# Convolution groups of twice the width, in the two small PSUM banks and in the PSUM pair of the output tile closed last

## The chip, the cores and the metric

The kernel runs on one core of a Trainium2 chip. A core has TensorE (PE in the profile, its weight loads PEld), VectorE (DVE), ScalarE (ACT), GpSimd (POOL) and SyncE (SP), which work through their own queues in order and wait for each other through semaphores, and 16 DMA engines. PSUM, into which TensorE writes, has 8 banks of 512 numbers of 32 bits in each of 128 partitions. The metric is the device time of one execution in microseconds (us); less is better.

## The reference

With S = 2048 rows, D = 576 channels and Dff = 4608:

```python
x = A_q
xn = _layernorm(x, axis=-1)
return x + _A_ref(xn, A_k, A_v, A_shift_k, A_ssm_k, A_ssm_D) + _B_ref(xn, B_w1, B_w2)

# A, of (q, k, v, shift_k, ssm_k, ssm_D), q being xn
k_shift = sum(k_pad[:, t:t + S, :] * shift_k[:, ks - 1 - t] for t in range(4))
kv = k_shift * v
y = causal_convolution_over_S(kv, ssm_k)      # per channel, through an FFT of length 2 S
A = q * (y + kv * ssm_D)

# B
h = maximum(einsum("bsd,df->bsf", x, w1), 0)
B = einsum("bsf,fd->bsd", h, w2)
```

(The two convolutions are written shorter here.) B is by far the larger part of the arithmetic; A's long convolution is a Fourier transform, a product and a way back, all as small matmuls.

## The kernel before

**Two streams on one TensorE.** The feed-forward part B is a fixed program: `QUADS` rounds (36), from the fourth on each a `quad` with seven products into the PSUM banks `psh` (tags h0, h1) and eight output units. The products come in the order 00, two units, 01, a rest, unit, s2, unit, s1, unit, s3, a rest, s4, two units, a rest, unit, 11, a rest. A product (`product`, L566) is two times three matmuls of 512 columns; a unit (`mm2`, L715) is 12 matmuls of 288 columns into a PSUM pair `pso`, two banks wide, which VectorE then adds to `acc` (L739; 21 units in the input stage are seeded by a ScalarE copy instead and copied back by it). `open_unit` (L707) opens the pair of the next unit before the matmuls of this one, so the two pairs take turns.

**The convolution** is a generator, `conv`, that is advanced between those pieces. `tick(cost)` (L1125) is called after each half of a product, each rest and each unit. It adds the cost to a clock, and while the convolution's clock is not behind it takes up to two steps, `next(stream)`. A step yields a weight (`W_FX` and the like), or a negative pause during which only B runs, so that transfers land. So the instructions of the convolution stand where tick happened to be called, in the middle of a product as well. `in_turn` (L750) holds its matmuls to this order on TensorE; `here` holds its copies behind the latest work of B on VectorE and ScalarE.

**Stages of the convolution**, each with 64-row matmuls in four quadrants (in the last, 128 rows by 64 columns) into the small banks `psf`, of which there are two (`fft_psum`):

- filter: 22 times `filter_group` of `KG` = 432 columns, through `group` (L807): matmuls into two banks, then a copy of one by ScalarE (L823) and of the other by VectorE (L825) into the ring `zs`, then stores to `zk` by SyncE (L861);
- input: 18 times `input_group` of `CW` = 512 columns, both copies by ScalarE, stores to `zx`; the rows before it are multiplied and gated on VectorE (`tap`, `gate`);
- frequency: for each of 18 pairs of chunks n a `spectrum` of the filter (four ScalarE copies, L994, then a swap of halves by DMA), a `product_of` (four VectorE multiplications, L1010, and a DMA into the one buffer `other`), a `join` (one VectorE instruction of 1024 columns, L1021, that reads `other`) and a `way_back` (two ScalarE copies, L1029, and stores to `zy`). In round n the order is spectrum n + 1, join n - 1, product n, way_back n - 1, with a weight yielded after the spectrum, the product and the way back;
- output: 16 tiles; two sets of matmuls of 288 columns, two `gate`s on VectorE (L1081), an `add` (L1088).

`Ring.put` gives the next of a few buffers; a buffer given again waits for its last readers.

## Time and profile before

| | |
|---|---|
| median of 3 runs | 1055.54 us (1054.64 to 1057.38) |
| the profiled execution's own time | 1057.48 us |
| its span in the profile | 1055.7 us |
| busy on VectorE | 700.0 us, 66% |
| busy on ScalarE | 435.6 us, 41% |
| busy on GpSimd | 464.4 us, 44% |
| line 752 on TensorE, the convolution's matmuls | 127.8 us, 1160 instructions |

The profile is one execution. In its rows "out<-in" are tiles (`psf` from `area`, the convolution's buffers; `pso` from `w` and `hh` or `ll`, a unit; `psh` from `x` or `xs` and a weight, a product), with partitions x columns. A matmul of the convolution (line 752) appears as two rows, one for each of two passes. Matmuls are pipelined, so a row's duration is longer than the distance to the next one: distances of starts are what counts on TensorE. An arrow in brackets says how long the engine had been idle and what ended that.

### The profile page before, as it was taken

The numbers are of one execution on the slowest core, as the hardware profiler recorded it, in microseconds if no ns is written. First come the engines' busy times: TensorE is split into PE (matmuls) and PEld (weight loads), VectorE is DVE, ScalarE is ACT, GpSimd is POOL, SyncE is SP. The second block draws the span as 40 slices with busy tenths as digits, with TensorE's granted clock in tenths as the row PEclk, the third lists the DMA queues.
The fourth block names the chain that finished last, engine by engine and source line by source line (L and its number), as shares of the span: only waits on it lengthen the run. The fifth ranks groups of instructions, "written<-read, shape, count | busy, mean of one in ns | idle before, by whom it ended". The sixth has DMA issues, their size and how long they took to land.

```text
span 1055.7 us, 17578 instructions
## 1 busy us (share of the span) xinstructions
PE 1038.6 (98%) x6506; PEld 844.5 (80%) x6506; DVE 700.0 (66%) x1083; ACT 435.6 (41%) x813; POOL 464.4 (44%) x502
## 2 busy tenths in 40 slices
PE   9999999999999999999999999999999999999997
PEld 5898999998877879888788888766766666678777
DVE  6787777774555547788778877456655566655765
ACT  7244334443435344444444444444344434433220
POOL 3335455555444354555454546423243224335351
PEclk9999999999999999999999999999999999999999
DMA  6114374579354563389942443597887677746785
GB/s 178 54 48 122 109 160 133 175 208 187 82 169 142 175 211 102 115 265 318 272 143 95 133 139 113 184 211 208 241 226 213 200 230 223 210 133 202 245 271 150
DMA packets 136321, 184.70 MB, mean 175 GB/s; under 512 B 70333, under 2 KB 88639, under 8 KB 135340
## 3 DMA queue, kind: packets, MB, share of 16 engines
q1 hardware_dynamic: 81652, 123.48, 39.3%
q0 software_dynamic: 16048, 52.44, 16.4%
q10 hardware_dynamic: 38536, 7.66, 3.8%
q8 instruction: 51, 0.84, 0.3%
q14 instruction: 34, 0.28, 0.1%
HBM read 119.04 MB, written 45.61 MB: 156 GB/s over the span
## 4 chain that ended last, share of the span: by engine, by line
PE 87%; DVE 5%; DMA 3%; ACT 2%; issue 2%; ACTq 1%; SPq 0%; DVEq 0%
PE pso L562 39%; PE psh L562 33%; PE psf L752 10%; PE psh_c L562 3%; DMA area<-area 2%; DVE area L1010 1%; DVE ll L586 1%; PE psw L1163 1%; DMA zk<-area 1%; DMA zy<-area 1%; DVE area L1021 1%; ACT area L994 1%; DVE acc L739 1%; ACTq L799 0%; DVE area L909 0%
## 5 line engine op out<-in xcount | busy, mean ns | idle before, releaser
L562 PE MATMUL pso<-w,hh 128*128 128x288 f32 x2304 | 468.0, 296 | 0.7 <-DVE acc L739 0.7
L562 PEld LDWEIGHTS pso<-w,hh 128*128 128x128 f32 x2304 | 378.4, 188 | 38.3 <-issue 10.8
L562 PE MATMUL pso<-w,ll 128*128 128x288 f32 x1152 | 339.4, 295 | 0.0
L739 DVE TENSOR_TENSOR acc<-pso,acc 128x576 f32<-128x576 f32 x243 | 183.0, 754 | 189.6 <-PE pso L562 189.2
L562 PEld LDWEIGHTS pso<-w,ll 128*128 128x128 f32 x1152 | 216.2, 188 | 0.0
L506 POOL TENSOR_TENSOR wb<-sums,wb 128x512 fp32r<-128x512 f32 x33 | 51.7, 1567 | 288.7 <-ACT wb L505 246.5
L506 POOL TENSOR_TENSOR w<-r,w 128x576 fp32r<-128x576 f32 x72 | 106.7, 1488 | 130.8 <-ACT w L505 130.8
L752 PE MATMUL psf<-area 64*64 64x512 f32 (+10 forms) x1160 | 127.8, 472 | 3.8 <-PE psh L562 1.4
L562 PE MATMUL psh<-x,wa 128*128 128x512 f32 x396 | 105.8, 399 | 3.3 <-ACT psh L641 3.2
L562 PE MATMUL psh<-xs,wb 128*128 128x512 f32 x396 | 106.2, 400 | 1.1 <-ACT u L656 1.1
L562 PEld LDWEIGHTS psh<-x,wa 128*128 128x128 f32 x396 | 71.5, 188 | 26.7 <-issue 9.1
L562 PEld LDWEIGHTS psh<-xs,wb 128*128 128x128 f32 x396 | 69.7, 188 | 26.5 <-issue 13.7
L562 PE MATMUL psh<-hl,wr 128*128 128x512 f32 x264 | 83.9, 399 | 0.4 <-ACT p L662 0.4
L506 POOL TENSOR_TENSOR wa<-r,wa 128x512 fp32r<-128x512 f32 x36 | 58.7, 1629 | 52.1 <-ACT wa L505 52.0
L586 DVE SCALAR_TENSOR_TENSOR ll<-psh,hh 128x512 fp32r<-128x512 f32 x66 | 45.2, 685 | 53.5 <-ACT hh L584 53.5
L752 PEld LDWEIGHTS psf<-area 64*64 64x64 f32 (+1 forms) x1160 | 39.6, 132 | 47.0 <-issue 25.2
L584 ACT ACTIVATE hh<-psh 128x512 fp32r<-128x512 f32 x66 | 39.5, 598 | 75.9 <-PE psh L562 75.7
L584 ACT ACTIVATE hh<-p 128x512 fp32r<-128x512 f32 x33 | 20.9, 632 | 103.0 <-DVE p L684 58.7
L677 DVE TENSOR_TENSOR u<-psh,u 128x512 f32<-128x512 f32 x33 | 22.8, 691 | 55.6 <-PE psh L562 53.0
L562 PEld LDWEIGHTS psh<-hl,wr 128*128 128x128 f32 x264 | 47.0, 188 | 14.6 <-issue 6.0
L679 ACT ACTIVATE psh<-psh 128x512 f32<-128x512 f32 x33 | 19.2, 582 | 93.9 <-DVE u L677 93.9
L562 PE MATMUL psh<-x,wc 128*128 128x512 f32 x198 | 53.9, 402 | 0.0
(127 smaller groups left out, 1454.3 us busy)
## 6 DMA issues: line engine op xcount, KB each, us to landing
r<-in_w POOLq DMA_DIRECT2D x70, 288.0 KB, 3.8
area<-area SPq DMA_DIRECT2D x144, 128.0 KB, 4.3
r<-in_w POOLq DMA_DIRECT2D x35, 512.0 KB, 4.6
area<-zk SPq DMA_DIRECT2D x18, 512.0 KB, 4.6
area<-zx SPq DMA_DIRECT2D x18, 512.0 KB, 3.3
zy<-area SPq DMA_DIRECT2D x36, 256.0 KB, 4.2
area<-zy SPq DMA_DIRECT2D x32, 288.0 KB, 5.0
zk<-area SPq DMA_DIRECT2D x42, 144.0 KB, 2.2
```

Of the source, the lines that this page charges most:

```text
L506: nc.gpsimd.tensor_tensor(w[:, 1, :n], src, w[:, 0, :n], OP.subtract)
L562: last = nc.tensor.matmul(ps, a, m, start=start and n == 0, stop=n == len(seq) - 1, skip_group_check=True)
L584: done["act"] = nc.scalar.activation(hh, ps, AF.Relu)
L586: nc.vector.scalar_tensor_tensor(ll, ps, 0.0, hh, op0=OP.max, op1=OP.subtract)
L677: nc.vector.tensor_tensor(u2, x, u2, OP.add)
L679: nc.scalar.activation(x, y, AF.Copy, scale=-1.0)
L739: done["acc"] = nc.vector.tensor_tensor(two(acc[t]), ps[:, :, :NH], two(acc[t]), OP.add)
L752: done["pe"] = nc.tensor.matmul(ps, a, m, start=start, stop=stop)
L994: nc.scalar.activation(filt[:, c, k, :], banks[k], AF.Copy)
L1010: nc.vector.tensor_tensor(filt[:, c, k, :], banks[k], filt[:, c, k, :], OP.mult)
L1021: nc.vector.scalar_tensor_tensor(filt, other, sign, filt, op0=OP.mult, op1=OP.add)
L1163: last = nc.tensor.matmul(idle[0], warm[:, :P], warm, start=True, stop=True)
```

## The change

`group` now takes two parts. The first goes into the two small banks as before, the second into a pair `psg` of the tag that held the output tile closed last (`borrowed`). The pairs `pso` get a tag each (`o0`, `o1`), and `slot` remembers which was opened and which closed last. Filter and input groups hold twice the columns: 11 and 9 of them, the last filter group shorter in its second part. In the frequency stage product n and spectrum n + 1 stand together, the spectrum in the borrowed pair, copied by two ScalarE instructions of 1024 columns instead of four of 512; way_back follows the product after 5.6 weights, not 3.6. In the output stage two tiles go together.

Before each such group the stream yields "wide"; `tick` then takes no step until it is called with `place` true, which is not so in the middle of a product and after a unit. The ring `zs` holds two wide buffers, the length of one group, instead of four half ones, of two groups. `terms` shrinks to one buffer, `sums` grows to four; the output stage has four rows of lookahead instead of three. A pair whose borrowed columns are fewer than a unit's is kept from being seeded (`unwritten`).

```diff
-    ps_o = ctx.enter_context(tc.tile_pool(name="ps_o", bufs=2, space=PSUM))
+    ps_o = ctx.enter_context(tc.tile_pool(name="ps_o", bufs=1, space=PSUM))
...
+    slot = {"open": 0, "closed": 0}
+    unwritten = set()
+
+    def borrowed():
+
+        return ps_o.tile([P, 2, 512], F32, tag=f"o{slot['closed']}", name="psg")
+
...
             matmuls(ps, ((h, hi), (h, lo), (l, hi)), start and c == 0)
-            tick(3 * W_MM)
+            tick(3 * W_MM, c == 1)
...
-        ps = open_ps[g, t] = ps_o.tile([P, 2, 512], F32, tag="o", name=f"pso{g}_{t}")
-        if seed:
+        slot["open"] = 1 - slot["open"]
+        ps = ps_o.tile([P, 2, 512], F32, tag=f"o{slot['open']}", name=f"pso{g}_{t}")
+        open_ps[g, t] = ps, slot["open"]
+        if seed and slot["open"] not in unwritten:
             seeded.add(t)
             nc.scalar.activation(ps[:, :, :NH], two(acc[t]), AF.Copy)
...
-        ps = open_ps.pop((g, t))
+        ps, slot["closed"] = open_ps.pop((g, t))
+        unwritten.discard(slot["closed"])
...
-        tick(W_UNIT)
+        tick(W_UNIT, False)
...
-        zs = Ring(*views(Z, 4, CW))
+        zs = Ring(*views(Z, 2, 2, CW))
...
+        def group(parts, engines):
+
+
+            wide = borrowed()
+            sets = [[fft_psum() for _ in range(2)], [wide[:, r, :] for r in range(2)]]
+            ends = []
+            for pieces, banks in zip(parts, sets):
+                off = 0
+                for w, mat, src in pieces:
+                    for k in range(2):
+                        for r in range(2):
+                            in_turn(banks[r][sides[r ^ k], off:off + w],
+                                    mat(r)[sides[r], A1 * (r ^ k):A1 * (r ^ k) + A1],
+                                    src[sides[r]], off == 0, True)
+                    off += w
+                ends.append(off)
+            if ends[-1] < NH or len(ends) == 1:
+                unwritten.add(slot["closed"])
+            outs = []
+            for n, off in enumerate(ends):
+                out = zs.put(("z", n))
+                outs.append([out[:, r, :] for r in range(2)])
+                if n and engines == ("act", "act"):
+                    with here():
+                        nc.scalar.activation(out[:, :, :off], wide[:, :, :off], AF.Copy)
+                    continue
+                for r in range(2):
+                    with here():
+                        if engines[r] == "act":
+                            nc.scalar.activation(out[:, r, :off], sets[n][r][:, :off], AF.Copy)
+                        else:
+                            nc.vector.tensor_copy(out[:, r, :off], sets[n][r][:, :off])
+            return outs
...
-            while starts and min(starts[0] + KG, flat) <= e * NH + (e == A2 - 1) * NH:
+            while starts and min(starts[0] + 2 * KG, flat) <= e * NH + (e == A2 - 1) * NH:
+                yield "wide"
                 filter_group(starts.pop(0))
-                yield W_FK / 2 / (len(range(0, flat, KG)) / A2)
+                yield W_FK / 2 / (len(range(0, flat, 2 * KG)) / A2)
...
-        sums = Ring(*rows[11:14])
-        terms = Ring(*rows[14:16])
+        sums = Ring(*rows[11:15])
+        terms = Ring(*rows[15:16])
...
-                    while made_groups < n_groups and (made_groups * CW + CW - 1) // D <= last:
+                    while made_groups < n_groups and (2 * CW * (made_groups + 1) - 1) // D <= last:
+                        yield "wide"
                         input_group(made_groups)
                         made_groups += 1
-                        yield W_FX
+                        yield 2 * W_FX
...
+        def second_spectrum(n):
+            wide = borrowed()
+            return spectrum(n, [wide[:, k, :] for k in range(2)], lambda to: [(to, wide)])
 
         def product_of(n):
 
             banks = [fft_psum() for _ in range(2)]
             turn(banks, [(0, raw["x"][n])])
             filt = filters[n]
+            leave = second_spectrum(n + 1) if n + 1 in pairs_n else lambda: None
...
+            leave()
...
-        spectrum(0)
+        first_spectrum()
         yield W_FMK
         for n in range(NCH // 2 + 1):
             if n + 1 in pairs_n:
-                spectrum(n + 1)
-            if n <= NCH // 2:
-                yield W_FMK
+                yield "wide"
             if n:
                 join(n - 1)
-            if n == NCH // 2:
-                yield W_FMX
             if n in pairs_n:
                 product_of(n)
-                yield W_FMX
+            yield W_FMK / 2 + W_FMX
             if n:
                 way_back(n - 1)
-                yield W_FMB
+                yield W_FMK / 2 + W_FMB
...
-        for i, t in enumerate(order):
-            y = ys.put(i)
-            banks = [fft_psum() for _ in range(2)]
+        for i in range(0, T, 2):
+            yield "wide"
+            wide = borrowed()
+            sets = [[fft_psum() for _ in range(2)], [wide[:, h, :] for h in range(2)]]
+            y = {j: ys.put(j) for j in (i, i + 1)}
+            for j, banks in zip(y, sets):
+                for h in range(2):
+                    for u in range(U):
+                        in_turn(banks[h][halves(u)[0], :NH], invs[j][:, u, :],
+                                zos[j, u][:, h * NH:(h + 1) * NH], True, True)
             for h in range(2):
-                for u in range(U):
-                    in_turn(banks[h][halves(u)[0], :NH], invs[i][:, u, :],
-                            zos[i, u][:, h * NH:(h + 1) * NH], True, True)
-            for h in range(2):
-                gate(i, h, banks[h], y)
-            load_z(i + 3)
-            yield W_FO / 2
-            add(i, y)
-            load_rest(i + 3)
-            yield W_FO / 2
+                gate(i, sets[0][h][:, :NH], y[i], h)
+            gate(i + 1, wide[:, :, :NH], y[i + 1])
+            for j in y:
+                load_z(j + 4)
+            yield W_FO
+            for j in y:
+                add(j, y[j])
+                load_rest(j + 4)
+                yield W_FO / 2
...
-    def tick(cost):
+    def tick(cost, place=True):
 
         if clock["done"] or clock["ffn"] < clock["until"]:
             clock["ffn"] += cost
             return
         clock["ffn"] += cost
         clock["conv"] += rate * cost
-        for _ in range(2):
-            if clock["conv"] < 0:
-                return
+        steps = 2
+        while steps and clock["conv"] >= 0 and (place or not clock["wide"]):
+            clock["wide"] = False
             try:
                 c = next(stream)
             except StopIteration:
                 clock["done"] = True
                 return
-            if c < 0:
+            if c == "wide":
+                clock["wide"] = True
+            elif c < 0:
                 clock["until"], clock["conv"] = clock["ffn"] - c, 0.0
                 return
-            clock["conv"] -= c
+            else:
+                clock["conv"] -= c
+                steps -= 1
```

Three places of the order that this gives. On TensorE in round 11 of B, the first filter group; `psh_2` is the product s2, `pso_3` the unit behind it. Before:

```order
L562 MATMUL psh_2_2925<-xs_706,wb_2886 128x512 x3
L752 MATMUL psf<-area 64x288 x4
L752 MATMUL psf<-area 64x144 x4
L562 MATMUL psh_2_2925<-xs_706,wb_2886 128x512 x3
L562 MATMUL pso_3_2981<-w_2760,hh_0_0_2741 128x288 x2
```

And now:

```order
L569 MATMUL psh_2_2925<-xs_706,wb_2886 128x512 x6
L762 MATMUL psf<-area 64x288 x4
L762 MATMUL psf<-area 64x144 x4
L762 MATMUL psg<-area 64x144 x4
L762 MATMUL psg<-area 64x288 x4
L569 MATMUL pso_3_2981<-w_2760,hh_0_0_2741 128x288 x2
```

The group has left the middle of the product for its end, and the one that followed a unit later stands directly behind it, in `psg`.

On ScalarE in round 17, where an input group meets the end of product s4; `psh17_4<-psh17_2` and `hh17_0_1` are B's own work behind that product, `hh17_1_1` comes after the next two units. Before:

```order
L679 ACTIVATE psh17_4_4947<-psh17_2_4756 128x512
L584 ACTIVATE hh17_0_1_4949<-u2_17_4863 128x512
L823 ACTIVATE area_1173<-psf_4967 128x512
L823 ACTIVATE area_1173<-psf_4968 128x512
L584 ACTIVATE hh17_1_1_5003<-p5_17_4894 128x512
```

And now:

```order
L686 ACTIVATE psh17_4_4948<-psh17_2_4743 128x512
L591 ACTIVATE hh17_0_1_4950<-u2_17_4834 128x512
L846 ACTIVATE area_1173<-psf_4916 128x512
L846 ACTIVATE area_1173<-psf_4917 128x512
L841 ACTIVATE area_1173<-psg_4915 128x1024
L591 ACTIVATE hh17_1_1_4988<-p5_17_4866 128x512
```

The copy of the borrowed pair is the third of the group's copies, and B's two instructions stand ahead of all three.

On TensorE in the frequency stage, rounds 26 and 27 before, round 26 now: `psh_4` is product 11, `psh_1` is product 00 in the first piece and 01 in the second, `pso_15` and `pso_10` are units. Before, two of the stage's sets, each an entry of its own:

```order
L562 MATMUL pso_15_7530<-w_7160,ll_1_1_7227 128x288
L752 MATMUL psf<-area 64x512 x4
L562 MATMUL psh_4_7495<-x_5041,wc_7323 128x512 x6
L562 MATMUL psh_4_7495<-hl_5045,wr_7236 128x512 x2
L562 MATMUL psh_1_7605<-x_4766,wa_7443 128x512 x3
L752 MATMUL psf<-area 64x512 x4
L562 MATMUL psh_1_7605<-x_4766,wa_7443 128x512 x3
```

And now a product with the next spectrum:

```order
L569 MATMUL psh_1_7264<-x_4796,wa_7088 128x512 x6
L762 MATMUL psf<-area 64x512 x4
L762 MATMUL psg<-area 64x512 x4
L569 MATMUL psh_1_7264<-hl_4907,wr_7232 128x512 x2
L569 MATMUL pso_10_7301<-w_7037,hh_0_0_7019 128x288 x2
```

The way back follows behind the second unit after it, alone in `psf`.

More of the change, by code (lines that the diff above doesn't have):

```diff
@@ L264, in block_xT @@
     def block_xT(pool, b, names, tags, xn):
-        wide = [ps_o.tile([P, 2, 512], F32, tag="o", name=f"psx{b}{k}") for k in range(2)]
+        wide = [ps_o.tile([P, 2, 512], F32, tag=f"o{k}", name=f"psx{b}{k}") for k in range(2)]
         ps = [wide[c // 2][:, c % 2, :] for c in range(4)] + [fft_psum()]
@@ L751, in in_turn @@
         with tc.issue_after(done["pe"].ins):
-            done["pe"] = nc.tensor.matmul(ps, a, m, start=start, stop=stop)
+            done["pe"] = nc.tensor.matmul(ps, a, m, start=start, stop=stop, skip_group_check=True)
     sides = (slice(0, 64), slice(64, P))
@@ L937, in stages @@
         yield -PAUSE / 2
-        n_groups, made_groups = T * D // CW, 0
+        n_groups, made_groups = T * D // (2 * CW), 0
         for t in range(T):
```

130 lines of the change are left out of this document (61 added, 69 removed).

## The prediction

> **What bounds the kernel now.** I read the page's first two parts and the chain first: which engine is never idle, and whether the last work hangs on it.
>
> ```profile
> span 1055.7 us, 17578 instructions
> PE 1038.6 (98%) x6506; PEld 844.5 (80%) x6506; DVE 700.0 (66%) x1083; ACT 435.6 (41%) x813; POOL 464.4 (44%) x502
> PEclk9999999999999999999999999999999999999999
> PE 87%; DVE 5%; DMA 3%; ACT 2%; issue 2%; ACTq 1%; SPq 0%; DVEq 0%
> ```
>
> TensorE is busy 98% of the span at an undiminished clock, and 87% of the chain is its own matmuls, one after the other. So the end moves by what TensorE saves or loses, and a transfer or a copy counts only where TensorE comes to wait for it. Busy is no proof of full speed, so next I read TensorE by stages of the convolution: filter, input (two rows), frequency, output. Each row has busy us of PE, PEld, DVE, ACT and POOL.
>
> ```profile
> 287.00:385.00 98.00, 98.00 (x794) 77.81 (x794) 53.43 (x93) 43.92 (x83) 44.76 (x56) 1.00 0.51 162
> 385.00:550.00 165.00, 162.07 (x1034) 140.43 (x1034) 127.25 (x177) 75.40 (x138) 86.16 (x83) 1.00 0.65 207
> 550.00:680.00 130.00, 129.19 (x838) 110.38 (x837) 96.67 (x132) 58.95 (x109) 68.16 (x66) 1.00 0.40 129
> 680.00:950.00 270.00, 264.98 (x1571) 185.39 (x1570) 158.25 (x232) 117.25 (x223) 92.37 (x96) 1.00 0.75 209
> 950.00:1042.00 92.00, 92.00 (x563) 72.58 (x562) 62.02 (x98) 21.36 (x39) 39.01 (x50) 1.00 0.70 221
> ```
>
> The frequency stage (680 to 950) has the most idle, 270.00 - 264.98 = 5.0 us; the first input row has 2.9, the others next to none. Everything else is hidden inside "busy", so I looked at the timeline of TensorE around one turn of the convolution, and at a stretch without one. Columns: start, duration, engine, line, instruction, times.
>
> ```profile
> 414.21 1.54 PE L562 MATMUL psh<-xs,wb 128*128 128x512 f32 x6
> 415.59 0.63 PE L562 MATMUL psh<-hl,wr 128*128 128x512 f32 x2
> 710.68 0.29 PE L562 MATMUL pso<-w,ll 128*128 128x288 f32 x1
> 710.90 1.09 PE L752 MATMUL psf<-area 64*64 64x512 f32 x8
> 711.92 1.66 PE L562 MATMUL psh<-xs,wb 128*128 128x512 f32 x6
> 713.42 0.42 PE L562 MATMUL pso<-w,hh 128*128 128x288 f32 x2
> 300.46 0.96 PE L752 MATMUL psf<-area 64*64 64x144 f32 x16
> 301.35 0.53 PE L562 MATMUL pso<-w,hh 128*128 128x288 f32 x2
> 709.38 1.59 PE pso L562 x12
> ```
>
> The last row, from the chain, is one output unit: 12 matmuls in 1.59 us, 0.13 each. Undisturbed, six 512-column matmuls take 415.59 - 414.21 = 1.38, 0.23 each.
>
> **The change part by part.** *Fewer turns.* The cost of one entry of the convolution follows from these rows in three pieces. Entry: the last unit matmul starts at 710.68 and would be followed 0.13 later, at 710.81; the turn starts at 710.90, so 0.09. Inside: the turn holds TensorE for 711.92 - 710.90 = 1.02. Its own streaming comes from mean durations by width:
>
> ```profile
> L752 PE MATMUL psf<-area 64*64 64x288 f32 x168 | 14.5, 416 | 0.0
> L752 PE MATMUL psf<-area 64*64 64x144 f32 x176 | 9.9, 295 | 0.0
> ```
>
> (416 - 295) / 144 = 0.84 ns per column and pass, and each product appears as two instructions: 512 x 2 x 0.84 = 0.86 us, with four quadrants side by side. That leaves 0.16. Exit: six matmuls take 713.42 - 711.92 = 1.50 for 1.38, so 0.12. One entry costs 0.09 + 0.16 + 0.12 = 0.37 us over its arithmetic.
>
> By the loops of the code there are 110 entries before: 22 filter, 18 input, 54 frequency, 16 output. In the changed order I count 65, since 45 sets in the borrowed pair stand directly behind a set in the small banks (11 filter, 9 input, 17 frequency, 8 output). The columns multiplied are the same. What has to be bounded is the seam between the two sets. The filter turn at 300.46 has such a seam inside (144 and 288 columns) and takes 0.89 for 432 x 2 x 0.84 = 0.73: again 0.16, nothing for the seam. Ends: a free seam saves 0.37, a seam that costs a whole entry saves nothing. I take the free one, by the row: 45 x 0.37 = **16.6 us saved**.
>
> The Trainium skill, "TensorEngine Tiling (Array Packing)", section Tiling Modes, says that changing the tiling mode, and not just the tile, drains TensorE. By that rule the sum stays 16.6, since a seam changes the tile alone; if every change of tile drained, it would be 0, and the turn at 300.46 speaks against that.
>
> *The frequency stage's waits.* Where turns take longer than 1.02, way_back waits:
>
> ```profile
> 680.00:950.00 270.00, 68.17 (x432) 14.05 (x432) 1.00 0.75 209
> 730.21 1.09 PE L752 MATMUL psf<-area 64*64 64x512 f32 x8
> 735.26 1.08 PE L752 MATMUL psf<-area 64*64 64x512 f32 x4 [1.24 <-issue]
> 736.50 1.08 PE L752 MATMUL psf<-area 64*64 64x512 f32 x4 [0.16 <-DVE area L1010]
> 733.89 2.47 DVE L1010 TENSOR_TENSOR area<-psf,area 128x512 f32<-128x512 f32 x4
> L1010 DVE TENSOR_TENSOR area<-psf,area x72: 673/678/692, 691.5 to 933.3; 128x512 f32<-128x512 f32 x72
> 702.38 1.43 DVE L1021 SCALAR_TENSOR_TENSOR area<-area,sign 128x1024 f32<-128x1024 f32 x1 [5.67 <-DMA area<-area]
> 705.14 0.97 PE L562 MATMUL psh<-x,wa 128*128 128x512 f32 x3 [1.37 <-ACT psh L641]
> ```
>
> The first row is line 752 alone: 68.17 us of busy for 54 turns that should take 54 x 1.09 = 58.9, so 9.3 us of waiting counted as busy; with the 5.0 idle, 14.3. The next three rows show the kind: a product ends its turn at 731.23, and the way back at 735.26 waits 1.24 and then splits, its second bank held until VectorE's four multiplications (2.47) release it. The row after them gives first and last of all 72 multiplications, the last two rows are another kind: VectorE stood 5.67 us at the first join for the transfer into "other", and TensorE 1.37 behind it. So about 14.3 - 1.4 = 12.9 is of the first kind.
>
> Now the product yields W_FMK/2 + W_FMX = 5.6 before way_back, not 3.6. The multiplications run from 691.5 to 933.3, 17 rounds of 10.5 weights: 1.35 us a weight, so the distance grows from 4.9 to 7.6 us. VectorE needs 2.47, a join of 1.43 and an accumulation of 0.75: it fits. In the order two rounds keep only some 3.7 us between product and way_back; I leave them 1.0 each, and 1.4 for unlike cases. Ends: 0 to 12.9 regained; I take **9.5**.
>
> *The wait that is added.* The next unit but one opens in the borrowed pair and waits until ScalarE (VectorE in the output stage) has emptied it. In the order 37 of 45 groups have a product, a rest or more than one unit in between, 2.0 to 5.7 us; eight have only one unit, 1.59: 2 filter, 2 input, 3 frequency, 1 output. Durations:
>
> ```profile
> 722.27 1.56 PE L562 MATMUL psh<-xs,wd 128*128 128x512 f32 x6
> 724.67 0.58 ACT L679 ACTIVATE psh<-psh 128x512 f32<-128x512 f32 x1 [2.45 <-DVE u L677]
> 725.16 0.62 ACT L584 ACTIVATE hh<-u 128x512 fp32r<-128x512 f32 x1
> L296 ACT ACTIVATE xf<-psx 128x1024 f32<-128x1024 f32 x4 | 4.0, 1022 | 0.2 <-DVE x L287 0.2
> L823 ACT ACTIVATE area<-psf 128x512 f32<-128x512 f32 x36 | 19.3, 590 | 3.6 <-PE psf L752 3.0 <-ACT wc L505 0.7
> L823 ACT ACTIVATE area<-psf 128x432 f32<-128x432 f32 x21 | 11.0, 523 | 22.4 <-PE psf L752 17.4 <-issue 4.0 <-ACT wc L505 0.5
> L870 ACT ACTIVATE area<-area 128x288 f32<-128x288 f32 x16 | 11.6, 722 | 9.5 <-DVE area L842 4.7 <-PE psf L752 4.5
> L677 DVE TENSOR_TENSOR u<-psh,u 128x512 f32<-128x512 f32 x33 | 22.8, 691 | 55.6 <-PE psh L562 53.0
> L739 DVE TENSOR_TENSOR acc<-pso,acc 128x576 f32<-128x576 f32 x243 | 183.0, 754 | 189.6 <-PE pso L562 189.2
> ```
>
> Six of the eight stand at the end of product s4 (psh from wd). That product ended at 722.27 + 1.38 = 723.65 here, and ScalarE had its two own instructions behind it done at 725.78: 2.1 us. In the changed order both stay ahead of the group's copies. A hand-over between engines is some 0.2, an estimate: 724.67 - 723.65 less the 0.69 of VectorE's addition (line 677) leaves 0.33 for two. Input: 2.1 + 2 x 0.59 + 1.02 = 4.3, with a hand-over 4.5; TensorE is there after 0.09 + 1.72 + 0.07 + 1.59 + 0.12 = 3.6: 0.9. Filter: 2.1 + 0.52 + 0.72 (a copy, line 870) + 0.52 + 0.2 = 4.1 against 3.4: 0.7, twice. Frequency: 2.1 + 2 x 1.02 + 0.2 = 4.3 against 3.6: 0.7, twice; and 0.6 at a product 00, where one ScalarE copy stands ahead. The second input case 0.1, output 0.2. Together **4.6 added**. Behind the waiting unit TensorE's whole queue stands. Ends: 0 and 45 x 0.8 = 36, if every group paid like these.
>
> The Trainium skill, "TensorEngine Tiling (Array Packing)", section Performance Considerations, warns that tiling speeds up TensorE but not the emptying of PSUM, which may become the bottleneck. By the rows ScalarE is busy 117.25 of 270 us in the frequency stage, so on the mean it isn't; by the rule it is at all 45 places, the 36 us above.
>
> *The first join.* Between product 0 and join 0 the order now has 5.6 weights instead of 7.6, 2 x 1.35 = 2.7 us less for the same transfer. Ends: 0 and 2.7; I take **2.0 added**, because the 5.67 above says that it was late already.
>
> *Stores.* A copy now waits for the stores of the group just before, not the last but one; they are twice as many.
>
> ```profile
> 289.83 93.87 SPq L861 DMA_DIRECT2D zk<-area  x86
> zk<-area SPq DMA_DIRECT2D x42, 144.0 KB, 2.2
> ```
>
> 86 stores in 93.87 us is at most 1.09 each, waits included; eight plus 2.2 to land make 10.9 us at most, and a wide filter group comes every 98 / 11 = 8.9. So ScalarE can be held up to 2 us, mostly with over 2.9 us until the pair is needed. In the input stage groups are over 11 us apart. Ends 0 and 8; I take **1.0 added**. Copies of 1024 columns instead of two of 512 (1.02 for 1.18), four rows of lookahead in the output stage, the single terms buffer (both its users are on VectorE, in order) and the unchanged 21 seeds I cost at nothing: other engines' work behind a busy TensorE.
>
> **Sum.** -16.6 - 9.5 + 4.6 + 2.0 + 1.0 = -18.5. The profiled execution took 1057.48 us (span 1055.7 and 1.8 around it): 1039.0. It lies 1.9 above the median of the runs, 1055.54, so for the median **1037 us**.
>
> **The rivals.** (1) *Handing back the pair is dearer than counted.* Some eighteen groups have under 3 us until reuse; with 0.8 at each, 14.4 instead of 4.6: 1047. For it: ScalarE's order is strict, and a late copy is late for all behind it. Against: mostly a product lies in between, and ScalarE is under half busy.
> (2) *The pairs don't act as one entry*, a wait on the borrowed bank or the late accumulation standing in each seam: no 16.6, 1053.6. Against: the accumulation is due 1.4 us or more before, and takes 0.75.
> (3) *Slower:* every group finds the pair late. At 0.8 each, 36 instead of 4.6: 1068. It decides from a mean wait of (18.5 + 4.6) / 45 = 0.51 us per group. For it: two wide copies take 2.04 us, more than a unit. This is where the rule of the Trainium skill on emptying PSUM ("TensorEngine Tiling (Array Packing)", Performance Considerations) would lead. Against: only eight places have just one unit between.
> (4) *All waits of way_back go and none comes back:* -16.6 - 12.9 + 1 = -28.5, 1027.
>
> **How the numbers follow.** Forecast (1027 to 1047) 0.74; rival 1, from 1047 to 1052, 0.11; rival 2 0.06; rival 3 0.04; beyond rival 4 0.05. About 0.3%, 3.2 us, is what a measurement here can tell from no change: below 1052.4 is faster, 0.74 + 0.11 + 0.05 = 0.90; rival 2 is the 0.06 of the same; rival 3 the 0.04 of slower. The range 1027 to 1049 holds the forecast and half of rival 1, 0.8.
>
> **What would show it.** Right: turns of 16 instructions without a gap in the seam; TensorE busy lower by about 26 us before new waits; way_back no longer split with "DVE" ahead; idle of a unit's weights ended by ScalarE's wide copies at about eight places. Wrong: idle in front of psg, many units released by ScalarE, VectorE held long at joins, or filter copies released by stores.

## The result

The changed kernel takes 1038.45 us (median of 6 runs, 1037.38 to 1043.4) against 1055.52 for the kernel before in the same session: a ratio of 0.9841, 95% interval 0.9819 to 0.9862. The forecast was 1037, with 1027 to 1049 around it. The execution that was profiled is the slowest of the six, 1043.4, 14.1 under the profiled execution of before; its trace is the one read here, and where it has more than the median has, the text says so.

First the page of the changed kernel, the same four lines as for before:

```profile
span 1041.6 us, 17492 instructions
PE 1020.0 (98%) x6506; PEld 848.8 (81%) x6506; DVE 704.6 (68%) x1075; ACT 430.2 (41%) x770; POOL 465.0 (45%) x502
PEclk9999999999999999999999999999999998999999
PE 30%; DMA 1%; DVE 1%; ACT 1%; issue 0%; SPq 0%; DVEq 0%; ACTq 0%
```

TensorE is still the bound. Two things are new: the clock line has an 8 in one of its 40 slices (859 to 885), and the chain covers only a third of the span, since it is followed back no further than to an instruction of VectorE at 692. Then the stages, with the same columns as before:

```profile
287.00:385.00 98.00, 96.74 (x806) 79.75 (x804) 57.21 (x95) 43.18 (x82) 45.32 (x56) 1.00 0.53 163
385.00:550.00 165.00, 159.63 (x1015) 140.42 (x1014) 126.55 (x175) 74.07 (x133) 86.73 (x82) 0.99 0.65 200
680.00:950.00 270.00, 263.90 (x1634) 196.41 (x1627) 161.78 (x240) 117.07 (x195) 96.01 (x101) 0.99 0.79 226
680.00:950.00 270.00, 54.80 (x432) 12.59 (x424) 0.99 0.79 226
773.26 1.09 PE L762 MATMUL psf<-area 64*64 64x512 f32 x8
774.17 1.04 PE L762 MATMUL psg<-area 64*64 64x512 f32 x8
775.14 0.53 PE L569 MATMUL pso<-w,hh 128*128 128x288 f32 x2
```

Idle of TensorE has not shrunk: 6.1 instead of 5.0 in the frequency stage, 5.4 instead of 2.9 in the first input row, 1.3 instead of none in the filter stage. What shrank is hidden in "busy". The fourth row is the convolution's line alone in the frequency stage: 54.80, and by the next three rows a pair is 774.17 + 1.04 - 773.26 = 1.95 as busy and a single turn 1.09, so 17 pairs and 20 single turns make 55.0. Nothing of the 9.3 that waited inside turns is left.

What TensorE waits for now is the list of its waits (what waits, for what, us in total, times, longest), first of before, then of the changed kernel, from 285 to 1042:

```profile
PE psh L562 <- ACT psh L641: 3.2, 2, 1.8
...
PE psh L562 <- ACT u L656: 1.1, 1, 1.1
PE pso L562 <- DVE acc L739: 0.7, 1, 0.7
PE psf L752 <- DVE area L1010: 0.7, 4, 0.2
```

```profile
PE pso L569 <- ACT area L1024: 4.5, 3, 4.0
PE pso L569 <- ACT pso L722: 3.8, 1, 3.8
PE psh L569 <- ACT psh L686: 1.7, 3, 1.2
PE pso L569 <- DVE area L848: 1.3, 2, 0.6
PE pso L569 <- ACT area L841: 1.2, 2, 0.9
```

Before, the quads wait for ScalarE here and there, and the convolution (psf) for its banks, until VectorE's multiplications (line 1010) have read them. After, it is a unit (pso) that waits until the borrowed pair has been emptied (lines 1024, 848, 841) or until its seed has been written (line 722). Two stops of some 4 us, at 856 and 385, make up most of it. The seven waits for emptying (3, 2 and 2 times) stand at the seven places with one unit that the prediction listed for the frequency, filter and input stages; at the eighth, in the output stage, nothing waits.

### The profile page after: what moved, and what is told of

Same layout as the page of the kernel before. It is cut to its first block, busy times and chain, and to the rows that moved or that the text cites. A ratio compares the mean times of both kernels' runs of the same rounds, so it can differ in the third digit from the quotient of the medians.

```text
span 1041.6 us, 17492 instructions
## 1 busy us (share of the span) xinstructions
PE 1020.0 (98%) x6506; PEld 848.8 (81%) x6506; DVE 704.6 (68%) x1075; ACT 430.2 (41%) x770; POOL 465.0 (45%) x502
## 5 line engine op out<-in xcount | busy, mean ns | idle before, releaser
L569 PE MATMUL psh<-x,wa 128*128 128x512 f32 x396 | 102.8, 395 | 0.5 <-ACT psh L648 0.4
L569 PE MATMUL psh<-xs,wb 128*128 128x512 f32 x396 | 102.7, 395 | 0.0
L569 PEld LDWEIGHTS psh<-x,wa 128*128 128x128 f32 x396 | 72.5, 188 | 16.8 <-ACT psh L648 1.3
L513 POOL TENSOR_TENSOR wa<-r,wa 128x512 fp32r<-128x512 f32 x36 | 56.6, 1572 | 47.6 <-ACT wa L512 47.6
L762 PE MATMUL psf<-area 64*64 64x512 f32 (+10 forms) x664 | 70.2, 489 | 0.0
L1051 DVE TENSOR_TENSOR area<-psf,area 128x512 f32<-128x512 f32 x72 | 44.8, 682 | 12.1 <-DMA area<-area 5.3
L512 ACT ACTIVATE w<-r 128x576 fp32r<-128x576 f32 x72 | 47.9, 680 | 10.6 <-DMA area<-in_v 7.4
L569 PE MATMUL psh<-x,wc 128*128 128x512 f32 x198 | 51.7, 396 | 0.0
```

What stands on the lines that cost most here:

```text
L512: nc.scalar.activation(w[:, 0, :n], src, AF.Copy)
L513: nc.gpsimd.tensor_tensor(w[:, 1, :n], src, w[:, 0, :n], OP.subtract)
L569: last = nc.tensor.matmul(ps, a, m, start=start and n == 0, stop=n == len(seq) - 1, skip_group_check=True)
L762: done["pe"] = nc.tensor.matmul(ps, a, m, start=start, stop=stop, skip_group_check=True)
L1051: nc.vector.tensor_tensor(filt[:, c, k, :], banks[k], filt[:, c, k, :], OP.mult)
```

## The experiments

Eleven variants and a second measurement of the changed kernel, each as a ratio to the kernel before, which was run beside it:

| run | what | us | ratio (95%) |
|---|---|---|---|
| again | the changed kernel | 1040.22 | 0.9854 (0.9832 to 0.9876) |
| back_alone | before, way back later | 1052.0 | 0.9959 (0.9946 to 0.9973) |
| old_back | changed, way back as before | 1045.87 | 0.9893 (0.9867 to 0.9919) |
| seam128 | a 128-row matmul in each seam | 1051.62 | 0.9957 (0.994 to 0.9974) |
| seam64 | a 64-row matmul in each seam | 1044.13 | 0.9896 (0.9865 to 0.9928) |
| no_close | no group at places with one unit | 1039.38 | 0.9822 (0.9796 to 0.9848) |
| anywhere | groups at any place | 1039.35 | 0.9841 (0.9817 to 0.9865) |
| join_late | join later, two buffers | 1042.82 | 0.9846 (0.9822 to 0.987) |
| loads_pool | first loads on GpSimd | 1032.52 | 0.9761 (0.9732 to 0.979) |
| before_pool | before, first loads on GpSimd | 1055.49 | 0.9992 (0.9982 to 1.0001) |
| pool_close | loads_pool and no_close | 1029.67 | 0.9746 (0.973 to 0.9761) |
| later_back | pool_close, way back later still | 1025.93 | 0.9701 (0.9681 to 0.9721) |

**Again.** No edit.

> The changed kernel once more, unaltered, for a profile of its own and as the base of the other runs. My theory (fewer entries 16.6, the way back's waits 9.5, less what the borrowed pair costs) gives 1038, ratio 0.984, and an idle of some 5 us spread over the places with one unit until reuse. If the two stops of TensorE of about 4 us in the profile of the change (at 385 and 856) belong to its order of work, they stand here again at the same places; if they are chance of the transfers, they are shorter or gone.

0.9854, in agreement with the first measurement. Both stops are there again, at the same instructions: 4.5 ahead of the unit that waits for its seed, 2.6 ahead of the unit behind the group at 856. They belong to the order of work; their length differs from one execution to the next.

**Is an entry worth 0.37?** A small matmul is set between the two sets of each pair, once over all 128 rows and columns of the array, as in the units, and once over 64 rows and 64 columns. The rows of the profile give this shape, the mode, as `128*128` or `64*64`. `64*64` is the mode of the sets in 37 of the 45 pairs; in the eight pairs of the output stage the sets are `128*64`, so there both matmuls break the seam. The same call stands in all three places that make pairs; one is shown.

```diff
+        def between(wide):
+            in_turn(wide[:, 0, :64], warm[:, :P], warm[:, :64], True, True)        # seam128
+            in_turn(wide[:64, 0, :64], warm[:64, :64], warm[:64, :64], True, True) # seam64
...
             for pieces, banks in zip(parts, sets):
+                if banks is sets[1]:
+                    between(wide)
                 off = 0
```

> The changed kernel with one small extra matmul over all 128 rows (bf16, 64 columns) in the seam between the two sets of each of the 45 pairs; nothing else is moved. My theory, an entry costs 0.37 whatever is done in it: 45 x 0.37 = 16.6 more than with the extra matmul in the mode of the sets (run seam64), and 45 x 0.03 to 0.1 for the extra matmul itself: 1056 to 1060. Rival, the gain is not from entries but from where and when they are let in: at most 45 x 0.1 = 4.5 more, 1038 to 1043, and no more than seam64.

> As seam128, but the extra matmul of each seam (bf16, 64 columns) uses 64 rows and 64 columns of the array, as the sets do. My theory: the seam stays free, only the extra matmul is paid, 45 x 0.03 to 0.1 = 1.4 to 4.5: 1040 to 1043. Rival, any change of tile or type in the seam drains TensorE as a whole entry does: 1054 and more, as seam128.

The timeline of TensorE at one pair, of seam128 and then of seam64:

```profile
776.37 1.09 PE L762 MATMUL psf<-area 64*64 64x512 f32 x8
777.39 0.20 PE L762 MATMUL psg<-warm 128*128 128x64 bf16 x1
...
778.54 0.54 PE L569 MATMUL pso<-w,hh 128*128 128x288 f32 x2
```

```profile
775.86 1.09 PE L762 MATMUL psf<-area 64*64 64x512 f32 x8
776.77 0.19 PE L762 MATMUL psg<-warm 64*64 64x64 bf16 x1
...
777.77 0.40 PE L569 MATMUL pso<-w,hh 128*128 128x288 f32 x1
```

From the pair's first instruction to the next unit it is 778.54 - 776.37 = 2.17 with the seam broken, 777.77 - 775.86 = 1.91 with the same matmul in the sets' mode, and 775.14 - 773.26 = 1.88 without one. Of the other pairs of this stage all of seam128 take 2.17 or 2.18; the filter and input stages show the same steps (1.92, 1.66, 1.62 and 2.18, 1.93, 1.89). So leaving the mode costs 0.26 here and staying in it 0.03: the seam is free, and rival 2 falls. (That it is 0.26 and not 0.37 would fit the exit's 0.12 being paid at a pair's end in either case; no run separates it.) The rule of the Trainium skill that the prediction weighed, "TensorEngine Tiling (Array Packing)", Tiling Modes, is borne out by these rows.

In the output stage the 64-row matmul leaves the mode too. One pair of the changed kernel, then one of seam64:

```profile
953.18 1.19 PE L762 MATMUL psf<-area 128*64 128x288 f32 x8
...
955.27 0.53 PE L569 MATMUL pso<-w,hh 128*128 128x288 f32 x2
```

```profile
950.93 1.19 PE L762 MATMUL psf<-area 128*64 128x288 f32 x8
952.05 0.21 PE L762 MATMUL psg<-warm 64*64 64x64 bf16 x1
...
953.32 0.53 PE L569 MATMUL pso<-w,hh 128*128 128x288 f32 x2
```

That is 2.39 against 2.09, so 0.30, and in seam128 it is 2.38. Seam64 therefore keeps 37 seams and breaks eight, which the expectation for it left out. Summed over the 45 pairs in this way, seam128 holds TensorE 12.5 longer than the changed kernel and 8.6 longer than seam64. In the time seam128 lies 11 to 12 above the changed kernel (by 0.0103 to 0.0116 of 1056), and 6 to 7 above seam64 (6.4 by the ratios, 7.5 by the medians); the intervals of these differences are some 3 to 4 us to either side. Within them a broken seam costs about its whole length. Seam64 holds TensorE 3.9 longer than the changed kernel, 2.3 of it in its eight broken seams, and takes 4 to 6 longer. Seam128 stayed below its expected 1056 to 1060 because a broken seam costs 0.26 and not 0.37.

**Is the way back's wait a term of its own?** Once without the pair, once undone in the changed kernel:

```diff
 back_alone (from the kernel before)
-                yield W_FMK
+                yield W_FMK / 2
             if n:
                 join(n - 1)
...
-                yield W_FMX
+            yield W_FMK / 2 + W_FMX
             if n:
                 way_back(n - 1)

 old_back (from the changed kernel)
-            yield W_FMK / 2 + W_FMX
+            yield W_FMX + (0 if n else W_FMK / 2)
             if n:
                 way_back(n - 1)
-                yield W_FMK / 2 + W_FMB
+                yield W_FMK + W_FMB
```

> The kernel before with one thing of the change: in the frequency stage 5.6 weights instead of 3.6 between a product and the way back, 2.0 instead of 4.0 ahead of the join; spectrum, groups and PSUM are those of before. My theory: the way back's waits are a term of their own, 9.5 less, 1046, ratio 0.991; no turn of a way back is split any more. Rival, the whole gain comes from fewer entries and where they are let in: no change, 1055, ratio 1.000. Rival, the whole gain is this shift: 1038, ratio 0.984.

> The changed kernel with one thing undone: in the frequency stage 3.6 weights between a product and the way back again (6.9 behind it), the spectrum still in the borrowed pair. Base is the changed kernel run again, 1040.2. If the shift is what rid the way back of its waits, turns of the way back are split again and TensorE loses some 10 to 13: 1050 to 1053. If it is the two small banks that the spectrum no longer uses, no change: 1039 to 1042. The shift alone, without the pair (run back_alone), moved the wait from the way back to the product's turn, which then waited for ScalarE's copies of the spectrum; so I expect that both are needed, and the first result.

Back_alone is 4.0 faster than before, not 9.5; old_back is 4 to 5.5 slower than the changed kernel (0.9893 against 0.9841 and 0.9854), not 10 to 13. The shift matters and is not the whole gain, but its size was half of what had been expected. The convolution's line in the frequency stage of back_alone, then of old_back, and a row of back_alone's timeline (TensorE's weight load):

```profile
680.00:950.00 270.00, 64.90 (x432) 13.65 (x432) 1.00 0.74 216
```

```profile
680.00:950.00 270.00, 61.19 (x432) 14.21 (x424) 1.00 0.79 225
```

```profile
700.05 0.19 PEld L752 LDWEIGHTS psf<-area 64*64 64x64 f32 x4 [0.52 <-ACT area L994]
```

In back_alone 64.90 - 54 x 1.09 = 6.0 of waiting is left in the turns, and it has changed its place: not the way back waits for VectorE, but the product for ScalarE's copies of the spectrum (line 994), which now stand only two weights ahead of it. With two small banks for three users a larger distance in one place is a smaller one in another. Only the pair, which takes the spectrum out of the small banks, leaves room for both: 54.80. In old_back 61.19 - 55.0 = 6.2 is back in the turns.

So the shift alone moves less waiting than expected, and what it moves shows in the time about whole. Old_back has 6.2 more in the turns and 1.0 less idle in this stage than the changed kernel (264.95 of the 270 busy, against 263.90), 5.2 together, and takes 4 to 5.5 longer. For back_alone the fair base is before_pool (further down), which has the frequency stage of the kernel before and whose profiled execution is near the median: its turns wait 67.15 - 58.9 = 8.3 and TensorE stands idle 3.7 there, in back_alone 6.0 and 0.6. That is 5.3 less waiting, for a time that is 4.0 lower (2.9 to 5.7).

**Where the stops come from.** Four variants of the changed kernel (before_pool is the edit of loads_pool in the kernel before; join_late also has two buffers `other` in turn, and two instead of three for the way back's result to make room):

```diff
 no_close
-            tick(3 * W_MM, c == 1)
+            tick(3 * W_MM, c == 1 and place)     # place=False in products 00 and s4

 loads_pool
-                queues = (nc.sync if t > 1 else nc.scalar,) * 2
+                queues = (nc.sync if t > 1 else nc.gpsimd,) * 2
...
-                    nc.scalar.dma_start(w[1:A1, :], k[1, 0:A1 - 1, T + t, :])
-                    nc.scalar.dma_start(w[A1:, :], k[0, :, T + t, :])
+                    nc.gpsimd.dma_start(w[1:A1, :], k[1, 0:A1 - 1, T + t, :])
+                    nc.gpsimd.dma_start(w[A1:, :], k[0, :, T + t, :])

 join_late
-            if n:
-                join(n - 1)
             if n in pairs_n:
                 product_of(n)
-            yield W_FMK / 2 + W_FMX
             if n:
+                yield (W_FMK / 2 + W_FMX) / 2
+                join(n - 1)
+                yield (W_FMK / 2 + W_FMX) / 2
                 way_back(n - 1)
...

 anywhere
-            tick(3 * W_MM, c == 1)
+            tick(3 * W_MM)
...
-        tick(W_UNIT, False)
+        tick(W_UNIT)
```

> The changed kernel with the first loads of the input stage (k and v of t up to 1) issued by GpSimd instead of ScalarE. My theory: the stop of 4 to 5 at 385 stands because ScalarE's seed of a unit is queued behind two issues that take 6.4 together: it goes, 3 to 5 less than 1040.2, 1035 to 1037. Rival, the transfers themselves are late behind the stores of the filter stage, and VectorE's first taps then hold up TensorE instead: 1039 to 1042, with a new stop between 388 and 420.

> The kernel before with the first loads of the input stage on GpSimd, nothing else. If the stop at 385 is the change's own (the seed of a unit, which stands ahead of ScalarE's issues in the kernel before, comes behind them since the pair is borrowed), the gain is at most the 1.3 that TensorE stands at 388 there: ratio 0.998 to 1.000. Rival, the issues cost the kernel before as much, and the gain of run loads_pool has nothing to do with the change: ratio 0.991 to 0.994.

Loads_pool takes 8 to 10 off the changed kernel (0.9761 against 0.9841 and 0.9854), more than the 3 to 5 expected; before_pool takes nothing measurable off the kernel before. ScalarE's timeline around the stop, of before and of the changed kernel, shows why (ACTq is its sequencer, which issues transfers):

```profile
379.09 0.65 ACT L713 ACTIVATE pso<-acc 128x576 f32<-128x576 f32 x1
...
386.32 2.25 ACTq L157 DMA_DIRECT2D area<-in_v  x2
```

```profile
380.97 6.36 ACTq L164 DMA_DIRECT2D area<-in_v  x2
...
388.45 0.65 ACT L722 ACTIVATE pso<-acc 128x576 f32<-128x576 f32 x1
```

Both kernels hold ScalarE with issues until 387 or later. Before, the seed of the unit had been written at 379.09, ahead of them. In the changed kernel the same seed (the first of the 21, for unit 4 of this round) stands behind the issues, and TensorE waits 3.8 for it. So the stop is the change's own, though its cause is in code that the change doesn't touch. Why these two issues take 6.36 was not tried.

> The changed kernel, but a wide group may not enter at the ends of products 00 and s4, behind which one unit stands before the pair is used again. My theory, the pair is handed back late at these places alone: the waits of a unit for ScalarE's or VectorE's copies in the profile of the change (0.8, 0.8, 1.0, 0.55, 0.44, 0.45 and the long one at 856) go, nothing else moves: 4 to 9 less than 1040.2, 1031 to 1036. Rival, a group that is kept out there comes a product later and waits, or makes others wait, as long: 1039 to 1042.

At 0.9822 it lies 2 to 3 under the changed kernel, within the intervals: alone it can't be told from no gain. The execution that was profiled is the fastest of its five, 1032.25 where the median is 1039.38. Its whole list of waits, and the convolution's line in the frequency stage:

```profile
PE pso L569 <- ACT pso L722: 3.5, 1, 3.5
PE psh L569 <- ACT psh L648: 0.8, 3, 0.5
```

```profile
680.00:950.00 270.00, 59.49 (x436) 14.12 (x428) 1.00 0.79 226
```

The seven waits for the pair are all gone, as expected. But the rival was right too: 436 instructions are 54.5 turns, some 55.5 without waits, so 4.0 is back inside the turns. A group that is kept out comes one unit later, and its way back doesn't: the distance between the two has shrunk. (Run later_back, below, bears this out.)

> The changed kernel with the join moved from ahead of a product to 2.8 weights ahead of its way back, and two buffers other in turn (two instead of three of the way back's result make room). My theory: the long stops of TensorE in the frequency stage (856, 725, 691 in the profile of the change) begin with VectorE, which stands in the join for the transfer into other and keeps ScalarE from its copies: they go, 3 to 5 less than 1040.2, 1035 to 1037. Rival, the stop is ScalarE's own two wide copies at a place with one unit: at most 1 less, 1039 to 1041, with a stop of over 1.5 still at the same place.

No gain (0.9846), though VectorE never again stood in a join for a transfer. The long stop is gone from its place (0.3 remains there) and stands at 780, where ScalarE was held by another late transfer, one of weights:

```profile
778.78 0.63 ACT L512 ACTIVATE wa<-r 128x512 fp32r<-128x512 f32 x1 [2.65 <-DMA r<-in_w]
...
779.89 1.92 ACT L1024 ACTIVATE area<-psg 128x1024 f32<-128x1024 f32 x2
```

In exchange the way back's weight loads now wait for the later join, 2.2 in five places. So the join was the messenger. As I read it, what makes the stop is a place with one unit, where anything late ahead of ScalarE's wide copies reaches TensorE. My theory fell; the rival (ScalarE's two copies at such a place) is nearer, but it is not their 1.9 alone.

> The changed kernel, but the wide groups may enter behind units and in mid product too (no place is forbidden). In the order three groups then have 1.5 and five 2.2 until the pair is used again, where the changed kernel has eight of 1.5; but a group that stands right behind a unit must wait in its seam until VectorE has added that unit (0.75 and two hand-overs) while the first set takes 0.95. By the time until reuse: 2 to 4 less than the changed kernel, ratio 0.980 to 0.982. Rival, that letting them in only at ends of products is what makes the borrowing cheap: seams wait, ratio 0.990 or more, with idle ahead of psg ended by VectorE's addition in over ten places.

0.9841, the same as the changed kernel. That groups enter only at ends of products buys nothing measurable: fewer places have one unit, and in exchange psg waits for VectorE's addition of a unit, 1.6 in four places:

```profile
PE psg L762 <- DVE acc L749: 1.6, 4, 0.8
```

**Putting it together.**

> The changed kernel with both: the first loads of the input stage on GpSimd, and no wide group at the ends of products 00 and s4. In the order 44 of 45 groups then have 2.8 or more until the pair is used again, one has 1.9; before, eight had 1.5. Each alone gave 0.9761 (loads) and 0.9822 (places) of the kernel before, against 0.984 to 0.985 of the changed kernel. My theory, these are two kinds of stop, each followed by a stretch of lower granted clock: the gains add, 0.973, some 1028, with less than 3 of TensorE idle between 287 and 950. Rival, the second gain comes from the same stop at 385 or from the clock alone: 0.976, no better than the loads alone.

> Run pool_close with the way back 2.1 weights later (7.7 instead of 5.6 behind its product). In pool_close five turns of the way back still take 0.5 to 1.2 longer than their 1.02 (690, 704, 732, 787, 853), since a group that is kept out of a place comes later and its way back does not; together 4.7. In the order the nearest way back now has 4.8 instead of 1.3 behind its product, where VectorE needs 3.6. My theory, a wait of the way back is worth its length once the stops behind it are gone: 3 to 5 less, ratio 0.970 to 0.972, no turn split. Rival, as in runs old_back and back_alone half of such a wait comes back elsewhere: 0.973 to 0.975.

```diff
 later_back (pool_close is the edits of loads_pool and no_close together)
-            yield W_FMK / 2 + W_FMX
+            yield W_FMK / 2 + W_FMX + 2.1
             if n:
                 way_back(n - 1)
-                yield W_FMK / 2 + W_FMB
+                yield W_FMK / 2 + W_FMB - 2.1
```

Pool_close is faster than both parents' medians, though its interval touches that of loads_pool; with the way back moved, 0.9701 lies clear of all of them, by the ratios 15 to 16 under the changed kernel. The convolution's line in the frequency stage, of pool_close and then of later_back, and the longest of what is left of TensorE's waits in later_back:

```profile
680.00:950.00 270.00, 58.33 (x424) 14.16 (x424) 1.00 0.78 224
```

```profile
680.00:950.00 270.00, 56.34 (x440) 14.71 (x440) 1.00 0.80 227
```

```profile
PE psh L569 <- ACT psh L648: 0.8, 3, 0.5
PE pso L569 <- DVE area L1122: 0.4, 1, 0.4
```

At 1.09 a turn, 55 instead of 53 turns would make the second 2.2 longer; it is 2.0 shorter, so 4.2 of waiting went from inside the turns, and the time fell by 0.0045 of 1056, 4.8. Here too a wait removed was worth about its length; the interval of this difference is some 3 us to either side.

## Why the prediction was right

The time was right, 1037 against 1038.45, and the direction by its reasons. The terms were not all right, and errors on both sides cancelled: that the number came so near is luck in part.

*Fewer turns, 16.6 saved.* Right, as far as the runs show it. A pair holds TensorE 1.88 for 2 x 0.86 = 1.72 of streaming, so the 0.16 inside is paid once and the seam is free. Breaking the seams takes back 12.5 of TensorE's time, and the kernel is 11 to 12 slower; no run takes back the whole 16.6.

*The frequency stage's waits, 9.5 regained.* Too small. The turns wait for nothing any more, the whole 12.9 that I gave as the upper end. I left 3.4 of it to rounds that would still be close; I had not seen that the spectrum, gone from the small banks, loosens every round. The reason was incomplete as well: I gave the whole gain to the shift, and undoing the shift puts back only 6.2 in the turns and costs 4 to 5.5, while the shift without the pair leaves 6.0 of waiting in them. It takes both.

*The pair handed back late, 4.6 added.* The places were right, the largest was not. Seven of the eight wait, 1.3 in the filter stage (predicted 1.4), 1.2 in the input stage (1.0), 4.5 in the frequency stage (2.0): there two places wait 0.25 each and one 4.0. The step that failed is the duration ahead of the copies: I took ScalarE's queue from one undisturbed place, 2.1, and at 856 VectorE stood 4.94 in the join for a transfer that needed 8.1 instead of the usual 3.7 to land. The chain of waits has it, from the transfer to the unit:

```profile
846.69 8.12 DMA area<-area
854.94 1.28 DVE area L1063
856.94 0.69 DVE u L684
858.15 0.62 ACT hh L591
858.77 1.83 ACT area L1024 x2
860.65 3.25 PE pso L569 x12
```

With 7.0 / 45 = 0.16 per group rival 3 (0.51) was far off, and so was rival 1's eighteen places. The warning of the Trainium skill that the emptying of PSUM may become the bound ("TensorEngine Tiling (Array Packing)", Performance Considerations) holds at these seven places and not on the mean.

*The seeds, costed at nothing.* Wrong, and the largest of the terms that were named and costed at nothing: one of the 21 seeds came behind ScalarE's issues, 3.8. I had counted the seeds, 21 before and after, and not looked where they stand in ScalarE's order.

*The first join, 2.0 added, and the stores, 1.0.* Both too dear. VectorE waited 0.53 at the first join, not the 5.67 of before, and the filter stage's copies waited for stores twice, at 318 and 353, where TensorE did not wait for them. Both are nothing in TensorE's list.

*What was not in the sum at all* is the clock. After each of the two long stops TensorE runs at a lower clock for a while. Two windows that hold these stretches, the granted clock third from the end:

```profile
388.00:393.00 5.00, 3.85 (x16) 3.72 (x17) 0.00 (x0) 2.72 (x6) 3.21 (x3) 0.66 0.58 167
859.00:868.00 9.00, 7.35 (x34) 6.42 (x34) 4.41 (x7) 2.40 (x4) 0.00 (x0) 0.62 0.68 163
```

5 x 0.34 = 1.7 and 9 x 0.38 = 3.4, together 5.1. In both cases the lower clock begins before the stop has ended, 0.27 and 0.74 ahead of it, so 0.5 of this falls where TensorE stood anyway, and 4.6 is lost.

Against the profiled execution: -16.6 - 12.9 + 7.0 + 3.8 + 4.6 = -14.1, less about 2.7 for waits of before that are shorter now (4.3 for lines 641 and 656, of which 2.1 stays at 686 and 648, and 0.7 elsewhere on its list) makes -16.8, where -14.1 was measured; 2.7 I can't place. I had -26.1 saved and +7.6 added; the trace has -29.5 and some +13 to 15. The predicted sum was near because I was too careful by 3.4 on the one side, and blind to more than that on the other. The profiled execution took 4.4 longer than the sum says; the median of the runs lies 5 lower than it, and of the other five executions no trace shows why.

## What to carry to other kernels

When work is moved into a resource that another stage hands over, list what stands in order ahead of the hand-over on the engine that frees it, transfers and issues included, and price a place by the slowest of these, not by an undisturbed one. Waits on one engine aren't independent: before a wait is priced as gone, ask where the edit moves it. In these runs what really left TensorE's rows showed in the time about whole, but the shift alone left 6.0 of 8.3 in the turns at another user of the banks, and the groups kept out of the close places put 4.0 into others. So after a change look at the list of waits again; here three small edits, two of them found in that list and the third in what the first two laid bare, were together worth nearly as much as the change.

## What the runs showed of the chip

A stop of TensorE can cost more than its length. The granted clock, in windows of 1 us (third from the end), after a stop of 1.88 in loads_pool that ends at 850.85; then in no_close after a stop of 3.48 that ends at 386.92:

```profile
851.00:852.00 1.00, 1.00 (x5) 1.00 (x6) 0.48 (x1) 0.00 (x0) 0.00 (x0) 0.50 0.88 201
...
853.00:854.00 1.00, 1.00 (x6) 1.00 (x6) 0.00 (x0) 0.00 (x0) 0.00 (x0) 0.50 0.27 57
854.00:855.00 1.00, 1.00 (x7) 0.87 (x6) 0.86 (x2) 0.00 (x0) 0.00 (x0) 0.85 0.31 74
```

```profile
387.00:388.00 1.00, 1.00 (x8) 1.00 (x9) 0.00 (x0) 0.13 (x1) 0.70 (x2) 1.00 0.37 130
```

After the shorter stop some 3.4 us go by at 0.50, a loss of 1.7; after the longer one nothing is lost. In the changed kernel 3.4 us at 0.50 go with the stop at 385, and 6.8 with the stop at 856. Two unit matmuls take 0.68 in such a stretch instead of 0.43.

The traces say which stops cost it. In each of them the granted clock changes only at steps of 3.41 us: in the changed kernel at 388.87, 392.29, 859.91 and 866.74, which are 1, 137 and 2 such steps apart. Cut along these steps, the stop of loads_pool lies in one of them, 847.47 to 850.89, which is idle for 1.88; the stop of no_close falls into two, 381.74 to 385.16 and 385.16 to 388.57, idle for 1.72 and 1.76. In all 14 traces, from 20 us on, every step at full clock with 1.81 or more of idle is followed by one at 0.50, and none with 1.80 or less is. A step at 0.50 is followed by another when 0.73 or more of it is idle (three cases, the stop at 856 among them, which reaches into it) and by the full clock at 0.30 or less. These bounds are read off these traces alone, from 29 steps of the first kind (14 of them at the end of an execution) and 18 of the second.

The Trainium skill, "TensorE: Matmul & The Clock Gate", in its part on the HAM clock gate, has half rate after an idle window of about 3.4 us, and says that the window runs freely. The length and the free run agree with the steps of these traces; that 1.88 of idle were enough does not agree with a whole idle window, and here the measurement decides.

So I would count a stop of TensorE as its length, and 1.7 more where some 1.8 of it may fall into one step; the stop at 856, which reached into the next, lost 3.0. Executions of one kernel differ in it: of no_close's five, the profiled one has a mean granted clock of 1.000 and took 1032.25, the other four 0.995 or 0.996 and 1036.32 to 1041.44. Loads_pool took a stop of 3.8 away and gained 8 to 10, of which the clock's 1.6 is one part and shorter waits further on another (its list of waits from 285 to 1042 adds up to 6.2, against 13.1 with the 3.8).
